# An SSM and feed-forward mix on one core: x's transposes in queues of their own, and a planner with measured durations

## The chip, the cores and the metric

The kernel runs on one core of one Trainium2 chip. Times are device microseconds of one execution; the time of a kernel is the median of its runs. Engines are named as in the profile: PE is TensorE, DVE VectorE, ACT ScalarE, POOL GpSimd, SP SyncE, which here issues the transfers.

## The reference

```python
def _A_ref(u, log_A_real, A_imag, C_real, C_imag, log_dt, D_skip):
    dt = jnp.exp(log_dt)
    A = -jnp.exp(log_A_real) + 1j * A_imag
    C = (C_real + 1j * C_imag) * dt[:, None]
    P = jnp.exp((A * dt[:, None])[:, :, None] * pos[None, None, :])
    K = 2.0 * jnp.einsum("dn,dnl->dl", C, P).real      # taps of a long filter
    ...                                                # y = u convolved with K along L, per channel
    return y + u * D_skip[None, None, :]

def _B_ref(x, w1, w2):
    return jnp.einsum("bsf,fd->bsd", jnp.maximum(jnp.einsum("bsd,df->bsf", x, w1), 0), w2)

x = A_u                                                # 1 x 2048 x 640, float32
g = _sigmoid((x * gate_w).sum(-1, keepdims=True))
return g * _A_ref(x, ...) + (1 - g) * _B_ref(x, w1, w2)   # w1 640 x 1728, w2 1728 x 640; N = 128
```

The convolution over 2048 positions is done with transforms of length 2048 in two factors, as products with tables.

## The kernel before

**Two halves of work, woven together.** The feed-forward half runs in three passes over the hidden columns (5, 5 and 4 blocks of 128, one of them 64 wide), and in each over eight groups of 256 rows of x. Products are made in float32 accuracy from a rounded high part and a low remainder of each operand: three products for one. In the first pass a group's x is loaded (`xu`), transposed on PE in three blocks of 2, 2 and 1 column tiles (`trans`, into the PSUM tile `pk`, of which there is one; for group 0 also `px`, `pg`), cast by ACT to the high part and subtracted by DVE to the low part (`xx`, two sets by turns), and stored to DRAM (`xt`) for the later passes. Then come the hidden products (`hidden` in the first pass, `wide` in the others: `pf<-xx,w1`), relu by ACT (`hh`) and its remainder by DVE (`hl`), and four runs of output products (`sums`: `pf<-w2,hh`, 320 wide), each evicted to `q`. Between passes q goes through DRAM (`part`): it is stored at a group's end and loaded again (`load_q`) in the next pass; there are two q buffers. In the last pass ACT first scales the loaded q by 1 - g (`q<-q,omg`), and what is finished goes to the output.

**The other half** makes the taps and convolves. 40 chunks of channels give phases and exponents on PE (`pg`, `px`, `pe`), then cosines, sines, exponentials and products on ACT and DVE (`cs`, `sn`, `mg`, `me`, `G`); two chunks together make taps on PE (`taps`, into `pk`), turned by DVE (`kt`), and stored (`kd`). The convolution then goes over five slices of 128 channels, in stages on PE, all into the PSUM tiles `pc`, of which there are three: `tf` (first factor of the transform, of the taps `ck`/`cl` and of the input `xu`), `tm`, pointwise products on ACT, DVE and POOL, `tn`, a turn on DVE (`relay`), and `tw`: eight products in four pairs for a slice (`inv1`). A pair is multiplied by the gate on ACT into one of five `yo` buffers, and either stored to DRAM (`y`), to be added to q later, or joined by POOL with what pass three has left in `part` (loaded as `yj`), and stored to the output.

**The planner.** No order is written out. Every step is a `Task` with an engine, a queue, a duration that the author estimates (`dur`), what it depends on, and tokens of the buffers that it takes. `Plan.run` simulates the engines with these durations and emits the program in the simulated order: tasks of one queue stay in the order in which they were added, and between the heads of an engine's queues the one with the lowest `rank` goes first among those that are ready. Transfers have one line of time, `dma`, that each moves on by its `kb` over a rate. A change of kind on PE (`mode`: 'f' for full products, 'c' for convolution, 't' for taps) costs `CHANGE`. On the chip the engines run by themselves: each takes its instructions strictly in the emitted order and waits at the one that isn't ready. All instructions are recorded by one helper, so all rows of the profile have its line, L314; the tile names tell what they are.

Of the kernel before, what the change touches and what calls it, by code (L numbers as in the profile page):

```python
# [51 lines left out]
GPR = 1  # L52
GTR = 3
# [88 lines left out]
class Plan:  # L142
# [5 lines left out]
    FETCH = 2.4  # L148
    BUSY = 2.6
    SLACK = .8  # L150
    BURST, GATHER, PATIENCE = ('c', 'c1'), 2, 3

    def __init__(self):
# [68 lines left out]
    def run(self):  # L222
        self.free = {e: 0.0 for e in self.LAG}
        mode, dma, log, done, block, since = {}, 0.0, [], 50.0, 0.0, 0.0
        heads = {k: 0 for k in self.queues}
        while True:
            best = None
            for e in self.LAG:
                c, soon = [], []
                for (eng, q), n in heads.items():  # L230
                    if eng == e and n < len(self.queues[eng, q]):
                        t = self.queues[eng, q][n]
                        r, known = self.ready(t)
                        for g in t.glue:
                            r2, k2 = self.ready(g)
                            r, known = max(r, r2), known and k2
                            for b in t.take:
                                k = sum(x.ring is b.ring for x in (*t.take, *g.take))
                                r = max(r, sorted(b.ring.slots)[k - 1] if len(b.ring.slots) >= k else 1e9)
                        (c if known else soon).append((r, t))  # L240
                if not c:
                    continue
                at = max(self.free[e], min(r for r, _ in c))
                key = lambda t: t.prio + (0.5 if t.mode is not None and mode.get(e) not in (None, t.mode) else 0)
                r, t = min((x for x in c if x[0] <= at), key=lambda x: key(x[1]))
                start = max(at, r)
                if e == 'PE' and mode.get(e) == 'f':


                    if t.mode in self.BURST and at - since < self.PATIENCE and self.burst(c, heads, at) < self.GATHER:  # L250
                        other = [x for x in c if x[1].mode == 'f' and x[0] <= at + .05]
                        if other:
                            r, t = min(other, key=lambda x: key(x[1]))
                            start = max(at, r)
                if e == 'PE' and (t.mode != 'f' or mode.get(e) != 'f'):

                    for r2, t2 in c:
                        if key(t2) < key(t) and r2 <= at + self.HOLD:
                            t, start = t2, max(at, r2)
                    hold = [r2 for r2, t2 in soon if t2.prio < t.prio and r2 <= at + self.HOLD]  # L260
                    if hold:
                        at = max(hold)
                if best is None or at < best[0]:
                    best = at, e, t, start
            if best is None:
                break
            _, e, t, start = best
            change = self.CHANGE.get(e, 0) if t.mode is not None and mode.get(e) not in (None, t.mode) else 0
            if e == 'PE' and t.mode != 'f':
                since = start + t.dur  # L270
            if t.mode is not None:
                mode[e] = t.mode
            for b in t.take:
                b.ring.slots.remove(min(b.ring.slots))
            t.fn()
            self.free[e] = start + change + t.dur
            if e == 'PE':

                done += t.n
                while done >= 128:  # L280
                    done -= 128
                    at = self.free[e] - t.dur * done / t.n
                    fetch = self.FETCH + (self.BUSY if dma > at + 2 else 0)
                    self.free[e] += max(0, block + fetch - at)
                    block = max(at, block + fetch)
            if t.port:

                self.free[e] += 0.25 * min(max(self.free['POOL'] - start, 0), t.dur)
            t.end = self.free[e] + t.lag
            if t.kb:  # L290
                dma = max(dma, start + min(t.dur, 0.62) + 0.5) + t.kb / (230 if start < 12 else 270)
                t.end = max(dma, start + t.dur) + 1.1
            for b in (*t.take, *t.use):
                b.left -= 1
                b.free = max(b.free, t.end)
                if b.left == 0:
                    b.ring.slots.append(b.free)
            heads[e, t.q] += 1
            log.append((start, t))
        stuck = [(k, self.queues[k][n]) for k, n in heads.items() if n < len(self.queues[k])]  # L300
        assert not stuck, [(k, len(self.queues[k]) - heads[k]) for k, _ in stuck]
        self.log = log
# [42 lines left out]
class Kernel:  # L345
# [30 lines left out]
    def feed_forward(self):  # L376
        A, nc, V, S, P, D_ = self.plan.add, self.nc, self.V, self.S, self.P, self.D
# [11 lines left out]
        parts, k = [], 0  # L389
# [5 lines left out]
        st = {}  # L395
# [90 lines left out]
        def trans(g, third, src):  # L486
            s_, ld = src
            bank = ('pk', 'px', 'pg')[0 if g else third]
            b_ = tok(bank)
# [18 lines left out]
            def low():  # L508
                V.tensor_sub(st['x', g][1][:, k0:k0 + kn], st.pop(('xb', g, third))[:, :kn],
                             st['x', g][0][:, k0:k0 + kn].bitcast(F32))  # L510
            a = A('PE', 'ff', 0.22 * kn, pe, [ld], take=[b_], use=[s_], mode='f')
            b = A('ACT', 'ff', 0.12 + 0.2 * kn, high, [a], take=[x_] if third == 0 else (),
                  use=[b_] if third == 0 else [b_, x_], rank=0)
            c = A('DVE', 'ff', 0.08 + 0.27 * kn, low, [b], use=[b_, x_], rank=0)
            X.setdefault((0, g), []).extend((b, c))
            self.x_read.append(a)

# [93 lines left out]
        def wide(p, P, f):  # L611
# [30 lines left out]
            def low():  # L642
                V.scalar_tensor_tensor(st['hw', f][1], st.pop(('hb', p, P, f)), 0.0, st['hw', f][0].bitcast(F32), op0=ALU.max,
                                       op1=ALU.subtract)
            wt, w_ = W[p, f, 0]
            ts = [A('PE', 'ff', 0.69, pe(k), [*wt, *xd_], take=() if k else [b_], use=[w_, *xs_] + ([b_] if k else []),
                    mode='f', n=3) for k in range(NT)]
            a = A('ACT', 'ff', 0.52, high, [*ts, *(self.zs if p == 1 and f > 1 else ())], take=[h_], use=[b_], rank=0)
            b = A('DVE', 'ff', 0.62, low, [a], use=[b_, h_], rank=0)
# [141 lines left out]
        for p, n in enumerate(PARTS):  # L791
# [3 lines left out]
            for k, g in enumerate(order):  # L795
# [28 lines left out]
                if not last:  # L824
                    es = [sums(p, g, j, q_, qld) for j in range(4)]

                    def store(p=p, g=g):
                        D_.dma_start(sc['part'][p % 2][g], st['q', g])
                    done[p, g] = A('SP', 'st', 0.62, store, es, use=[q_], kb=640, rank=6, late=True)
                    continue  # L830
                if k % 2 == 0 and k < 6:
                    paced = [x for i in order[k + 2:k + 4] for x in X[p, i]]
# [179 lines left out]
    def ssm(self, C=16):  # L1012
# [26 lines left out]
        st = {}  # L1039
# [25 lines left out]
        def phases(c):  # L1065
            p_, s_ = tok('pg'), tok('sc')
            rd, r_ = rows[c]

            def pe():
                p = self.psg.tile([128, 4, 256], F32, name="pg")  # L1070
                pf = p.rearrange("p d j -> p (d j)")
                st['pg'] = pf.rearrange("p (d j) -> p d j", j=64)
                for h in range(2):
                    x = slice(h * 512, h * 512 + 512)
                    self.E.matmul(pf[:, x], R[c], self.tg[:, x], start=True, stop=True)

            def whole():
                st['sc', c] = [st['gp'].tile([128, C, 64], F32, name=k, bufs=5) for k in ("sn", "cs")]
                S.copy(I(st['sc', c][1]), st['pg'])
            a = visit[c, 1] = A('PE', None, 0.5, pe, [rd, opened, *self.tg_done], take=[p_], use=[r_], rank=GPR, mode='f')  # L1080
            b = acts[c, 0] = A('ACT', None, 0.97, whole, [a], take=[s_], use=[p_], rank=2)
            d = A('DVE', 'g1', 1.14, lambda: V.tensor_sub(st['sc', c][0], st['pg'], I(st['sc', c][1])), [b],
                  use=[p_, s_], rank=G1R)
            e = A('DVE', 'g1', 0.62, lambda: V.tensor_scalar(I(st['sc', c][1]), I(st['sc', c][0]), 0x7fffffff, None,
                                                             op0=ALU.bitwise_and), [d], use=[s_], rank=G1R, port=True)
            tasks[c] = dict(s=s_, abs=e)

        def exponents(c):
# [13 lines left out]
            def exps(k):  # L1102
# [5 lines left out]
                        st['me', c] = st['gp'].tile([128, C, 32], F32, name="me", bufs=4)  # L1108
                        S.activation(st['me', c], st.pop(('pe', c)), AF.Exp)
                return go  # L1110
            a = visit[c, 2] = A('PE', None, 0.7, pe, [rd, opened, *self.tg_done], take=[p_], use=[r_], rank=GPR, mode='f')
            b = acts[c, 1] = A('ACT', None, 0.52, exps(0), [a], take=[m_], use=[p_], rank=2, mode='exp')
            d = acts[c, 2] = A('ACT', None, 0.96, exps(1), [b], use=[p_, m_], rank=2, mode='exp')
            s_ = tasks[c]['s']
# [39 lines left out]
        def taps(p):  # L1154
# [17 lines left out]
            def out():  # L1172
                kt = st.pop(('kt', p))
                for j in range(4):
                    d0 = 2 * (p * C + j * Q)
                    D_.dma_start(self.sc['kd'][:, d0:d0 + 2 * Q, :].rearrange("(h a) d b -> a h (d b)", h=2),
                                 kt[32 * j:32 * j + 32].rearrange("p h q b -> p h (q b)"))
            a = visit[p, 0] = A('PE', None, 2.0, pe, [*w[0]['f'], *w[1]['f']], take=[b_], use=us, rank=GTR, mode='t', n=128)
            b = A('DVE', 'g5', 0.65, turn, [a], take=[k_], use=[b_], rank=G5R)
            d = A('POOL', 'g5', 0.6, lambda: P.tensor_add(st['kt', p][:, 1, :, 0], st['kt', p][:, 1, :, 0], dsk[:, p]),  # L1180
                  [b, sk], use=[k_])
# [359 lines left out]
```

## Time and profile before

| | |
|---|---|
| median of 3 runs | 644.29 us (642.56 to 644.78) |
| profiled execution | 642.35 us, its span 640.6 us |
| PE, DVE, ACT, POOL busy | 617.3, 508.5, 402.1, 93.9 us |
| moved by DMA | 107.78 MB |

Of the span, roughly the first 95 us are pass one of the feed-forward half with the parameters of the taps on DVE; to some 405 us the taps are made beside passes one and two; from then on the convolution runs beside passes two and three. In a row of the timeline the time in brackets is how long the engine had been idle, and who ended that. PE's products overlap, so their own durations add up to more than the time they take; runs of them are read from the chain.

### The profile page before, as it was taken

The page shows a single profiled execution, that of the slowest core. Times are in us where ns is not written, and L with a number is a line of the kernel's source. Part 1 is how long each engine was busy: PE and PEld are TensorE (multiplying, and loading weights), DVE is VectorE, ACT ScalarE, POOL GpSimd, SP SyncE. Part 2 cuts the span into 40 slices and gives each one's busy share as a digit, 9 for nine tenths or more (in the row PEclk, how much of TensorE's full clock was granted, in tenths as well). Part 3 has the DMA queues.
Part 4 walks back from the last instruction along what each step waited for, and adds up shares of the span by engine and source line. Part 5 has one row for each costly group of instructions (what it writes and reads, how often), then busy time and mean ns, then how long its engine had stood idle before and what let it go on. Part 6 is the DMA issues. An engine that isn't in the chain of part 4 may idle for free.

```text
span 640.6 us, 19212 instructions
## 1 busy us (share of the span) xinstructions
PE 617.3 (96%) x8236; PEld 503.0 (79%) x8236; DVE 508.5 (79%) x818; ACT 402.1 (63%) x603; POOL 93.9 (15%) x134
## 2 busy tenths in 40 slices
PE   7989999899999899999999999999999999999897
PEld 6989998798898798898898898665565556756577
DVE  4889936989999999998999999768579753966542
ACT  5557439999999988988978985113443424432550
POOL 0000000000000000000000000024151531713633
PEclk9999999999999999999999999999999999999999
DMA  9974774333456734373454225794406558156355
GB/s 256 326 236 147 221 229 165 105 125 112 136 167 210 255 122 144 122 242 117 129 198 154 79 80 176 258 315 132 144 3 215 185 164 263 53 158 188 102 166 133
DMA packets 76176, 107.78 MB, mean 168 GB/s; under 512 B 7610, under 2 KB 58682, under 8 KB 75195
## 3 DMA queue, kind: packets, MB, share of 16 engines
q1 hardware_dynamic: 75930, 106.14, 53.2%
q8 instruction: 65, 1.06, 0.7%
q10 hardware_dynamic: 160, 0.41, 0.3%
q14 instruction: 21, 0.16, 0.1%
HBM read 67.47 MB, written 44.30 MB: 174 GB/s over the span
## 4 chain that ended last, share of the span: by engine, by line
PE 56%; DVE 5%; DMA 2%; ACT 2%; issue 1%; SPq 1%; DVEq 0%; ACTq 0%
PE pf L314 35%; PE pc L314 13%; PE pk L314 4%; DVE ku L314 3%; PE pg L314 2%; PE px L314 2%; DMA part<-q 1%; ACT ku L314 1%; PE pe L314 1%; DMA out_dram<-yo 1%; SPq L314 1%; DVE sn L314 1%; ACT cs L314 0%; DVE q L314 0%; ACT q L314 0%
## 5 line engine op out<-in xcount | busy, mean ns | idle before, releaser
L314 PE MATMUL pf<-xx,w1h 128*128 128x256 f32 (+1 forms) x760 | 184.2, 339 | 0.4 <-DVE xx L314 0.3
L314 PEld LDWEIGHTS pf<-xx,w1h 128*128 128x128 f32 x760 | 125.2, 189 | 22.8 <-issue 7.3
L314 PE MATMUL pf<-xx,w1l 128*128 128x512 f32 (+1 forms) x340 | 115.7, 340 | 0.0
L314 PE MATMUL pf<-w2h,hh 128*128 128x320 f32 x288 | 89.7, 315 | 2.4 <-DVE hl L314 1.5
L314 PE MATMUL pf<-w2l,hh 128*128 128x320 f32 x288 | 87.8, 309 | 0.0
L314 ACT COPY ku<-pc 128x512 f32<-128x512 f32 (+1 forms) x60 | 43.8, 761 | 68.2 <-PE pc L314 56.7
L314 PE MATMUL pf<-w2h,hl 128*128 128x320 f32 x256 | 73.3, 312 | 0.0
L314 PEld LDWEIGHTS pf<-xx,w1l 128*128 128x128 f32 x340 | 64.3, 189 | 7.6 <-DVE w1l L314 0.2
L314 POOL TENSOR_TENSOR kt<-kt,dsk 128x8 f32<-128x8 f32 x20 | 10.3, 515 | 392.7 <-DVE kt L314 377.8
L314 POOL TENSOR_TENSOR ku<-ku 128x256 f32<-128x256 f32 x80 | 56.2, 737 | 55.3 <-DVE ku L314 49.1
L314 DVE TENSOR_TENSOR ku<-pc,ku 128x512 f32<-128x512 f32 x80 | 52.6, 684 | 12.5 <-ACT ku L314 11.3
L314 DVE STREAM_TRANSPOSE ku<-pc 128x512 f32<-128x512 f32 x80 | 50.2, 683 | 13.7 <-PE pc L314 13.7
L314 PEld LDWEIGHTS pf<-w2h,hh 128*128 128x128 f32 x288 | 54.1, 188 | 7.7 <-issue 3.7
L314 DVE TENSOR_TENSOR sn<-pg,cs 128x1024 f32<-128x1024 f32 x40 | 48.7, 1217 | 7.5 <-ACT cs L314 7.5
L314 PEld LDWEIGHTS pf<-w2l,hh 128*128 128x128 f32 x288 | 54.1, 188 | 0.6
L314 ACT ACT_TABLE_LOAD x42 | 53.9, 1283 | 0.7
L314 ACT CAST cs<-pg 128x1024 int32<-128x1024 f32 x40 | 40.3, 1008 | 21.2 <-PE pg L314 21.0
L314 DVE TENSOR_TENSOR mg<-mg,cs 128x1024 f32<-128x1024 f32 x40 | 48.9, 1222 | 1.3
L314 PEld LDWEIGHTS pf<-w2h,hl 128*128 128x128 f32 x256 | 46.4, 188 | 3.5 <-issue 2.9
L314 PE MATMUL pc<-ku,tm 64*32 64x256 f32 x1280 | 42.2, 392 | 3.6 <-DVE ku L314 2.4
L314 ACT ACTIVATE cs<-cs,half_pi 128x1024 f32<-128x1024 f32 x40 | 45.6, 1140 | 0.0
L314 ACT ACTIVATE hh<-pf 128x512 fp32r<-128x512 f32 (+1 forms) x40 | 20.5, 513 | 39.4 <-PE pf L314 39.4
(170 smaller groups left out, 1232.5 us busy)
## 6 DMA issues: line engine op xcount, KB each, us to landing
xx<-xt SPq DMA_DIRECT2D x24, 640.0 KB, 6.8
xt<-xx SPq DMA_DIRECT2D x16, 640.0 KB, 3.9
part<-q SPq DMA_DIRECT2D x16, 640.0 KB, 3.4
q<-part SPq DMA_DIRECT2D x16, 640.0 KB, 5.3
ws<-in_B_w_dram SPq DMA_DIRECT2D x20, 320.0 KB, 5.5
kd<-kt SPq DMA_DIRECT2D x80, 64.0 KB, 1.8
ub<-in_A_u_dram SPq DMA_DIRECT2D x10, 512.0 KB, 4.7
xu<-ub SPq DMA_DIRECT2D x5, 1024.0 KB, 6.2
```

Source lines behind the costliest of these rows:

```text
L314: self._last = self._tc.keep_in_program_order(f(*a, **k))
```

## The change

The three steps of `trans` move from the queue `ff`, in which they stood in one order with all products, casts and remainders of the feed-forward half, to a queue `xp` on each of PE, ACT and DVE; on PE with rank 4.5, while the products have 5. So a block of transposes is placed as soon as the simulation has its inputs and the buffer `pk` ready, wherever the products are. The other edits change numbers of the simulation: durations on PE of a wide product (0.69 to 0.681), of phases (0.5 to 0.46), exponents (0.7 to 0.69) and taps (2.0 to 1.83), half the cost of a change of kind that involves taps, and the transfers: a task of several transfers is now simulated as so many, each 0.62 us after the other, with rates by queue instead of 270 (230 in the first 12 us), and 1.27 us to land instead of 1.1.

```diff
+    RATE = dict(x=330, q=287, st=320, yq=200, y4=260, mx=297, cu=215, kd=231, ub=401, xt=485, rows=697, prm=215, tab=340, tab0=171)
...
+            if e == 'PE' and 't' in (t.mode, mode.get(e)):
+                change /= 2
...
             if t.kb:
-                dma = max(dma, start + min(t.dur, 0.62) + 0.5) + t.kb / (230 if start < 12 else 270)
-                t.end = max(dma, start + t.dur) + 1.1
+                m = max(1, round(t.dur / 0.625))
+                for j in range(m):
+                    dma = max(dma, start + 0.62 * j + 1.15) + t.kb / m / self.RATE.get(t.q, 250)
+                t.end = max(dma, start + t.dur) + 1.27
...
-            a = A('PE', 'ff', 0.22 * kn, pe, [ld], take=[b_], use=[s_], mode='f')
-            b = A('ACT', 'ff', 0.12 + 0.2 * kn, high, [a], take=[x_] if third == 0 else (),
+            a = A('PE', 'xp', 0.22 * kn, pe, [ld], take=[b_], use=[s_], rank=4.5, mode='f')
+            b = A('ACT', 'xp', 0.12 + 0.2 * kn, high, [a], take=[x_] if third == 0 else (),
                   use=[b_] if third == 0 else [b_, x_], rank=0)
-            c = A('DVE', 'ff', 0.08 + 0.27 * kn, low, [b], use=[b_, x_], rank=0)
+            c = A('DVE', 'xp', 0.08 + 0.27 * kn, low, [b], use=[b_, x_], rank=0)
...
-            ts = [A('PE', 'ff', 0.69, pe(k), [*wt, *xd_], take=() if k else [b_], use=[w_, *xs_] + ([b_] if k else []),
+            ts = [A('PE', 'ff', 0.681, pe(k), [*wt, *xd_], take=() if k else [b_], use=[w_, *xs_] + ([b_] if k else []),
...
-                    done[p, g] = A('SP', 'st', 0.62, store, es, use=[q_], kb=640, rank=6, late=True)
+                    done[p, g] = A('SP', 'st', 0.62, store, es, use=[q_], kb=310, rank=6, late=True)
...
-            a = visit[c, 1] = A('PE', None, 0.5, pe, ...
+            a = visit[c, 1] = A('PE', None, 0.46, pe, ...
...
-            a = visit[p, 0] = A('PE', None, 2.0, pe, ...
+            a = visit[p, 0] = A('PE', None, 1.83, pe, ...
```

Since the simulation sets the whole order, nearly every row of every engine moves a little. Three places follow.

**DVE in the first pass, at the subtractions for group 2 before and group 3 now** (`xx` is a subtraction of x's remainder, `hl` one of the hidden layer, `ra` and `sa` steps of the parameters' exponential, `logit` the gate's sum). Before:

```order
L314 SCALAR_TENSOR_TENSOR sa<-sa,ra 128x640 x2
L314 SCALAR_TENSOR_TENSOR hl_560<-pf,hh_559 128x512
L314 TENSOR_TENSOR xx<-pk,xx 128x512
L314 SCALAR_TENSOR_TENSOR sa<-sa,ra 128x640
L314 SCALAR_TENSOR_TENSOR hl_587<-pf,hh_586 128x256
L314 TENSOR_TENSOR xx<-pk,xx 128x256
```

Now:

```order
L319 SCALAR_TENSOR_TENSOR hl_597<-pf,hh_596 128x256
L319 SCALAR_TENSOR_TENSOR ra<-ni,ra 128x640
L319 TENSOR_SCALAR sa<-ra 128x640
L319 TENSOR_TENSOR xx<-pk,xx 128x512
L319 SCALAR_TENSOR_TENSOR sa<-sa,ra 128x640 x4
L319 TENSOR_TENSOR xx<-pk,xx 128x512
L319 SCALAR_TENSOR_TENSOR sa<-sa,ra 128x640 x2
L319 SCALAR_TENSOR_TENSOR xu,logit<-xu,gw 128x640
L319 TENSOR_TENSOR xx<-pk,xx 128x256
```

Before, each subtraction of x came behind the remainder of the hidden block that was made beside it; now group 3's three stand among the parameter steps, while PE makes the output products of group 1. On PE the blocks of transposes stand accordingly: before between hidden products, 30 and 15 of them apart, now between output products. This is the first block of group 3 now (`w2h,hl` and the like are output products):

```order
L319 MATMUL pf<-w2h_276,hl_512 128x320
L319 MATMUL pf<-w2h_299,hl_564 128x320
L319 MATMUL pk<-ident,xu 128x128 x4
L319 MATMUL pf<-w2h_314,hl_564 128x320
L319 MATMUL pf<-w2h_351,hl_597 128x320
```

Before, the last block of a group stood behind its last hidden products and ahead of the first output products.

**SP in the last pass, at the end of group 4** (`part_4<-q` is its second store, `q<-part_6` the load of group 6 into the same buffer, `yj` loads for the joins). Before:

```order
L314 DMA out_dram<-q 64x256 x2
L314 DMA part_4_72<-q 128x384
L314 DMA yj<-part_4_72 128x2x128
L314 DMA yj<-part_0_68 128x2x128
L314 DMA yj<-part_1_69 128x2x128
L314 DMA yj<-part_2_70 128x2x128
L314 DMA yj<-part_3_71 128x2x128
L314 DMA q<-part_6_82 128x1280
```

Now:

```order
L319 DMA part_4_72<-q 128x384
L319 DMA yj<-part_4_72 128x2x128
L319 DMA q<-part_6_82 128x1280
L319 DMA yj<-part_0_68 128x2x128
L319 DMA yj<-part_1_69 128x2x128
L319 DMA out_dram<-yo 64x4x128 x2
L319 DMA yj<-part_2_70 128x2x128
```

The load of q has moved ahead of four loads of yj.

**ACT at the multiplications of the `tw` products of slices 2 and 3** (`yo<-pc,gate`, four rows to a pair; `ku<-pc` are casts of other convolution stages). Before:

```order
L314 COPY ku<-pc 128x4x128x2 x4
L314 ACTIVATE yo<-pc,gate 128x128 x24
L314 COPY ku<-pc 128x512 x3
L314 ACTIVATE q<-q,omg 128x640
L314 COPY ku<-pc 128x512
L314 ACTIVATE q<-q,omg 128x640
L314 COPY ku<-pc 128x512 x4
L314 ACTIVATE yo<-pc,gate 128x128 x8
```

Now:

```order
L319 COPY ku<-pc 128x4x128x2 x4
L319 ACTIVATE yo<-pc,gate 128x128 x12
L319 ACTIVATE q<-q,omg 128x640
L319 ACTIVATE yo<-pc,gate 128x128 x12
L319 ACTIVATE q<-q,omg 128x640
L319 ACTIVATE yo<-pc,gate 128x128 x8
L319 COPY ku<-pc 128x512 x6
```

The two scalings of group 6's q stood between casts of the `tm` stage; now they stand inside the multiplications. On PE the `tw` products, before 6, 2, 4 and 4 rows for these two slices with other work between, are now 6 and 10, with 20 output products between:

```order
L319 MATMUL pf<-w2h_5350,w2l_7315 128x320
L319 MATMUL pc<-ku,tw 64x512 x10
L319 MATMUL pc<-ck,tf 64x512 x4
L319 MATMUL pc<-xu,tf 64x512 x16
L319 MATMUL pc<-cl,tf 64x512 x4
```

For slices 0 and 1 it is the same (before 6, 2, 4 and 4, now 6 and 10).

More of the change, by code (lines that the diff above doesn't have):

```diff
@@ L1079, in whole @@
                 S.copy(I(st['sc', c][1]), st['pg'])
-            a = visit[c, 1] = A('PE', None, 0.5, pe, [rd, opened, *self.tg_done], take=[p_], use=[r_], rank=GPR, mode='f')
+            a = visit[c, 1] = A('PE', None, 0.46, pe, [rd, opened, *self.tg_done], take=[p_], use=[r_], rank=GPR, mode='f')
             b = acts[c, 0] = A('ACT', None, 0.97, whole, [a], take=[s_], use=[p_], rank=2)
@@ L1110, in exps @@
                 return go
-            a = visit[c, 2] = A('PE', None, 0.7, pe, [rd, opened, *self.tg_done], take=[p_], use=[r_], rank=GPR, mode='f')
+            a = visit[c, 2] = A('PE', None, 0.69, pe, [rd, opened, *self.tg_done], take=[p_], use=[r_], rank=GPR, mode='f')
             b = acts[c, 1] = A('ACT', None, 0.52, exps(0), [a], take=[m_], use=[p_], rank=2, mode='exp')
@@ L1177, in out @@
                                  kt[32 * j:32 * j + 32].rearrange("p h q b -> p h (q b)"))
-            a = visit[p, 0] = A('PE', None, 2.0, pe, [*w[0]['f'], *w[1]['f']], take=[b_], use=us, rank=GTR, mode='t', n=128)
+            a = visit[p, 0] = A('PE', None, 1.83, pe, [*w[0]['f'], *w[1]['f']], take=[b_], use=us, rank=GTR, mode='t', n=128)
             b = A('DVE', 'g5', 0.65, turn, [a], take=[k_], use=[b_], rank=G5R)
```

## The prediction

> **What bounds the kernel now.** I read the page first: its span, its busy row and its clock row.
>
> ```profile
> span 640.6 us, 19212 instructions
> PE 617.3 (96%) x8236; PEld 503.0 (79%) x8236; DVE 508.5 (79%) x818; ACT 402.1 (63%) x603; POOL 93.9 (15%) x134
> PEclk9999999999999999999999999999999999999999
> ```
>
> TensorE (PE) is busy for 617.3 of 640.6 us at the full granted clock, and the change neither adds nor removes a product. So the time is PE's work plus what PE waits. The table of busy time by stage says who could make it wait (columns: window, PE, PEld, DVE, ACT, POOL busy with counts, clock, DMA share, GB/s):
>
> ```profile
> 0.00:40.00 40.00, 35.10 (x248) 32.95 (x248) 28.00 (x65) 20.06 (x38) 0.87 (x7) 1.00 0.95 281
> 160.00:200.00 40.00, 38.47 (x462) 34.57 (x460) 39.22 (x61) 37.44 (x50) 1.14 (x2) 1.00 0.56 174
> 560.00:600.00 40.00, 37.25 (x555) 20.98 (x553) 28.31 (x48) 15.45 (x40) 16.56 (x20) 1.00 0.54 157
> ```
>
> The first stage has slack on VectorE (DVE) and ScalarE (ACT), the tap stage has next to none (39.22 of 40 on DVE), the convolution has slack again but waits on chains through DMA. The view of waits, cut to PE, is the whole budget:
>
> ```profile
> PE pk L314 <- DVE xx L314: 5.6, 5, 1.7
> PE pc L314 <- DVE ku L314: 3.1, 6, 1.7
> PE pk L314 <- DMA xu<-in_A_u_dram: 2.3, 2, 1.1
> PE pg L314 <- DVE sn L314: 2.1, 1, 2.1
> PE pf L314 <- DVE hl L314: 1.5, 1, 1.5
> PE pe L314 <- POOL ident masks.py:199: 1.5, 1, 1.5
> PE pc L314 <- ACT ku L314: 1.0, 1, 1.0
> PE pf L314 <- ACT hh L314: 0.9, 1, 0.9
> ```
>
> These eight add up to 18.0 us. The 1.5 at the start and one of the two 1.1 on the first load stay in any order, so a reordering can win at most about 15 us; what it can lose has no such ceiling. Before and after, PE's order leaves its matrix products 37 times for convolution pieces and 20 times for taps, so switching costs the same.
>
> **Part 1: x's transposes in queues of their own.** The largest row above, 5.6 us in 5 waits, is one pattern. The timeline around the longest:
>
> ```profile
> 36.82 0.66 PE L314 MATMUL pk<-ident,xu 128*128 128x128 f32 x4
> 37.51 0.59 ACT L314 CAST xx<-pk 128x512 fp32r<-128x512 f32 x1
> 37.53 0.49 DVE L314 TENSOR_SCALAR sa<-ra 128x640 f32<-128x640 f32 x1
> 38.05 1.68 DVE L314 SCALAR_TENSOR_TENSOR sa<-sa,ra 128x640 f32<-128x640 f32 x2
> 39.66 0.68 DVE L314 SCALAR_TENSOR_TENSOR hl<-pf,hh 128x512 fp32r<-128x512 f32 x1
> 40.26 0.68 DVE L314 TENSOR_TENSOR xx<-pk,xx 128x512 fp32r<-128x512 f32 x1
> 40.99 0.44 PE L314 MATMUL pk<-ident,xu 128*128 128x128 f32 x2 [1.74 <-DVE xx L314]
> ```
>
> The buffer pk is single. The second block of transposes is cast by ACT at 37.51, but DVE subtracts only at 40.26, behind parameter steps (sa) and the hidden layer's hl. The third block stands 15 products further on PE: 40.99 - 1.74 - 36.82 = 2.43 us for four transposes and 15 products, so some 2.0 us of cover against a round trip of 40.94 - 37.2 = 3.7 us.
>
> In the new order the blocks of groups 3 to 7 stand among the output products of a group, 12, 16 and 19 of them apart. A run of such products gives the price:
>
> ```profile
> 623.67 13.12 PE pf L314 x88
> 620.01 3.65 PE pc L314 x16
> 603.34 2.02 PE pc L314 x124
> ```
>
> 13.12 / 88 = 0.149 us each, so the cover becomes 1.8, 2.4 and 2.8 us, where cast and subtraction alone are 0.59 + 0.68 and some 0.3 of hand-over, 1.6 us. For group 3, DVE now has the first xx, four sa steps (4 x 0.84 = 3.4, half of the 1.68 row each), then the second xx: ready about 5.9 us after the first block starts, with the third block due at 0.4 + 2.4 + 0.4 + 2.8 = 6.0 (0.4 for four transposes, 2.43 less 2.0 above). That just fits. I leave 0.8 of the 5.6 in place: -4.8 us. Bounds: 0 (the waits come back behind other DVE steps) to -5.6.
>
> Further waits of that stage:
>
> ```profile
> 13.47 0.63 PE L314 MATMUL pk<-ident,xu 128*128 128x128 f32 x4 [1.15 <-DMA xu<-in_A_u_dram]
> 99.31 0.41 PE L314 MATMUL pf<-w2h,hh 128*128 128x320 f32 x1 [0.89 <-ACT hh L314]
> 175.45 0.41 PE L314 MATMUL pf<-w2h,hh 128*128 128x320 f32 x1 [1.53 <-DVE hl L314]
> ```
>
> The first waits for group 1's load. Twelve more hidden products now stand ahead of it, 12 x 2.0 / 15 = 1.6 us, more than the wait: -1.1 (bounds 0, -1.15). The loads in SyncE's queue stand in the same order up to there. The other two are the step from a group's hidden products to its output products. At the later one a tap (2 us) now stands between most of the hidden products and the outputs, at the earlier one a phase product and a tap follow the first four. But at groups 2 and 3 the two transposes that stood in this step are gone and x's cast is ahead of the last hidden cast on ACT, which can cost some 0.5 each. Of 2.4 I take -1.0 (bounds +1, -2.4).
>
> **Part 2: the new costs in the tap stage.** Shorter phases, taps and products let the planner put more PE work ahead of each DVE step. Counted in PE's own work, the first convolution product comes about 6 us later than before; the last group's x blocks stand some 17 us earlier, out of the busiest stretch. DVE is at 39.22 of 40, so a late DVE step can hit PE anywhere; before, this happened once, at pg (2.1). I take -1.0 (bounds +3, -2.1).
>
> **Part 3: the convolution and its transfers.** The worst place of before:
>
> ```profile
> 583.35 3.49 SPq L314 DMA_DIRECT2D yj<-part  x5
> 586.94 0.54 SPq L314 DMA_DIRECT2D q<-part  x1
> 591.83 0.83 ACT L314 ACTIVATE q<-q,omg 128x640 f32<-128x640 f32 x1 [4.96 <-DMA out_dram<-yo]
> 592.56 0.56 ACT L314 COPY ku<-pc 128x512 f32<-128x512 f32 x1
> 594.72 1.15 PE L314 MATMUL pc<-ku,tm 64*32 64x256 f32 x32 [1.70 <-DVE ku L314]
> ```
>
> SyncE issues five yj loads before group 6's q load; ACT's in-order queue stands 4.96 us at the scaling of q (the view names another transfer, the q load is what it reads); the casts behind it come late, and PE waits 1.70, then 0.50, 0.17 and 0.24 at the next steps. In the new order that q load stands behind one yj load instead of five, 4 x 0.7 = 2.8 us sooner, and no cast of that stage stands behind it: -2.6, and with the similar 1.0 at 457 us -3.6 (bounds 0, -4.4).
>
> What comes instead: the last convolution products (tw, four pairs for each of five slices) of slices 0 and 1, and of 2 and 3, now stand in one burst each, six and ten products with 20 output products between, and the scaling of q for groups 4 and 6 stands inside the burst in ACT's queue. Prices:
>
> ```profile
> 574.45 0.53 DVE q L314
> 576.53 6.80 DMA part<-q
> 621.19 3.21 ACT L314 ACTIVATE yo<-pc,gate 128x128 f32<-128x128 f32 x12 [1.83 <-PE pc L314]
> part<-q SPq DMA_DIRECT2D x16, 640.0 KB, 3.4
> q<-part SPq DMA_DIRECT2D x16, 640.0 KB, 5.3
> ```
>
> Group 6's q load needs the buffer of group 4, so it waits until group 4's last store has landed. From group 4's last product to that store's issue are 576.53 - 574.45 = 2.1 us and 0.1 before it, landing takes 3.4 (median) to 6.8 (here), two issues 1.2, the load 5.3: data at 12.0 to 15.4 us. PE gets there sooner: four products 0.6, the tn products 2.0, three pairs 3 x 0.91 (3.65 / 4) = 2.7, 20 products 3.0, buffer waits and switches about 0.9, then three more pairs into the three PSUM buffers: 12.0. The next pair needs a buffer that ACT empties only after scaling q (0.83) and four multiplications (3.21 / 3 = 1.07): at 13.9 to 17.3 instead of 12.0. So 1.9 to 5.3 us, in each of the two bursts. In slice 0's burst the scaling stands one pair later, but three yj loads stand ahead of its q load. I take 2.5 each, near the median landing, because fewer other transfers stand ahead of the store than at 576: +5.0. Bounds: 0 (the data is there) to +16, where the five yo buffers, freed only by stores behind these loads in SyncE's queue, add a few us to each.
>
> **Sum.** -4.8 - 1.1 - 1.0 - 1.0 - 3.6 + 5.0 = -6.5 us. Against the profiled execution's 642.35 us that is 635.9; that execution lies 1.9 us below the median of the three runs, 644.29, so I forecast **637.8** as median. The tail is as before: after the last tw products PE has 62 products (9.2 us) instead of 88, and ACT's 16 multiplications behind them take 4.4.
>
> **Rivals.** *A, slower: the bursts of tw products.* The same mechanism at its upper price, 8 us a burst instead of 2.5: group 4's store lands after 6.8 us as it did at 576, and the yo stores queue behind the yj loads on SyncE. -6.5 + 11 = +4.5, so 648.8. It decides from a landing of some 6 us on. For it: ACT did stand 4.96 us at just this scaling. Against: another such store, issued at 504.08, let its reader start at 508.90, as the transfers were fewer.
>
> ```profile
> 504.08 0.33 SPq L314 DMA_DIRECT2D part<-q  x1
> 508.90 1.88 SPq L314 DMA_DIRECT2D yj<-part  x3
> ```
>
> A wait of PE in one piece of over 3.4 us would, by the Trainium skill, "TensorE: Matmul & The Clock Gate", section "HAM oscillation", drop the clock to half for a window of 3.4 us, worth about 1.7 us more in each burst by an estimate from that page: 652 instead of 649. No wait of this trace is that long and its clock row never drops, so no run here shows it so far; I give it 3 of A's 20 in 100.
>
> *B, same: DVE takes it back.* The tap stage runs at DVE's pace, so PE time won before 160 us is waited away between 160 and 400 at pg, pk and pf: the gains of part 1 (6.9) vanish, the rest nets to +0.4, so 644.7. For: 39.22 of 40. Against: PE waited only 2.1 us in 200 us of that stage, as other products fill in, and the new order has those too.
>
> *C, better: the q data is in time and all waits of part 1 go.* -6.5 - 5.0 - 0.8 - 1.4 = -13.7, so 630.6. For: transfers are now costed nearer to what the page shows. Against: ACT is the slower one inside a burst anyway.
>
> That the change doesn't do what it says is excluded by the order: the transposes do stand elsewhere.
>
> **Numbers.** Forecast 0.50 (634 to 642), A 0.20, B 0.16, C 0.14. The range 630 to 647 takes in B and the upper half of C, and leaves out two thirds of A and C's lower half, 0.2 in all. About 0.3% (1.9 us) is what a measurement of this kernel can tell: faster is the forecast and C, 0.64; same is B, 0.16; slower is A, 0.20.
>
> **What would show it.** In the waits view "PE pk <- DVE xx" falls from 5.6 to under 1.5, and "DMA xu" to one wait of 1.1. The row at 594.72 has no successor: tm products run without a wait over 0.5. In the two bursts ACT stands before a scaling of q for 1 to 3 us and PE waits 2 to 4 us nearby. The step from hidden to output products costs 1 to 2 us in all. I am wrong if the first 160 us still hold 6 us of PE waits, if the bursts show none or over 5 us each, or if PE's waits between 160 and 400 us exceed 4 us.

## The result, and the profile after

The changed kernel takes 641.23 us (median of 22 runs) against 643.40 us for the kernel before (22 runs): a ratio of 0.997, 95% interval 0.9957 to 0.9983. That is 1.9 us less (1.1 to 2.8 by the interval) where I had forecast 6.5. The time itself lies inside the forecast's 634 to 642, but that is luck, as the band is wide: the change is about a third of what was forecast. The profiled execution took 640.79 us with a span of 639.0.

The first page of the changed kernel, span and busy row:

```profile
span 639.0 us, 19204 instructions
PE 619.6 (97%) x8236; PEld 504.4 (79%) x8236; DVE 508.8 (80%) x818; ACT 402.4 (63%) x603; POOL 93.2 (15%) x134
```

Its table of busy time by stage, the three stretches that were shown of before (columns: window, PE, PEld, DVE, ACT, POOL busy with counts, clock, DMA share, GB/s):

```profile
0.00:40.00 40.00, 37.68 (x267) 35.74 (x267) 28.29 (x69) 22.81 (x51) 0.87 (x7) 1.00 0.97 293
160.00:200.00 40.00, 39.06 (x566) 34.27 (x566) 38.98 (x55) 37.36 (x48) 1.84 (x3) 1.00 0.54 165
560.00:600.00 40.00, 36.83 (x494) 19.78 (x500) 24.15 (x41) 17.16 (x44) 12.43 (x14) 1.00 0.52 146
```

The first stage has gained (37.68 us busy instead of 35.10), the last has not. And PE is busy for 619.6 us instead of 617.3 with the same 8236 products, which the prediction had no term for. The view of waits, cut to PE (total us, times, longest), without the wait for ident that is unchanged; "issue" is a stop for which the profile names no releaser:

```profile
PE pc L319 <- ACT yo L319: 4.2, 3, 2.4
PE px L319 <- ACT mg L319: 2.3, 3, 1.2
PE pf L319 <- issue: 1.9, 1, 1.9
PE pf L319 <- DVE hl L319: 1.3, 3, 0.9
PE pf L319 <- DVE q L319: 1.1, 1, 1.1
PE pc L319 <- issue: 0.5, 1, 0.5
PE pk L319 <- DVE cs L319: 0.4, 1, 0.4
PE pc L319 <- DVE ku L319: 0.3, 2, 0.2
PE pf L319 <- DVE xx L319: 0.3, 1, 0.3
PE pk L319 <- DMA xu<-in_A_u_dram: 0.3, 1, 0.3
PE pk L319 <- DVE xx L319: 0.2, 1, 0.2
PE pk L319 <- DVE sn L319: 0.2, 1, 0.2
PE pc L319 <- ACT ku L319: 0.2, 1, 0.2
```

Of the rows that led before, xx, xu and ku are all but gone. The first row is the price of the bursts. Two things are new: a stop of 1.9 us with no releaser but "issue", and px waiting for ACT.

The first burst in the timeline, SyncE's queue, then ACT, then PE (columns: start, duration, engine; in brackets the idle time before and its releaser):

```profile
484.60 1.87 SPq L319 DMA_DIRECT2D yj<-part  x3
486.51 0.60 SPq L319 DMA_DIRECT2D q<-part  x1
492.89 0.83 ACT L319 ACTIVATE q<-q,omg 128x640 f32<-128x640 f32 x1 [1.86 <-DMA q<-part]
494.80 1.08 PE L319 MATMUL pc<-ku,tw 128*64 128x512 f32 x4 [2.38 <-ACT yo L319]
```

Three yj loads are issued ahead of the q load; ACT stands 1.86 us at the scaling of q, and PE 2.38 us behind ACT, inside the burst. The other burst, at 574 to 578 us, costs 1.17 and 0.66.

The stop without a releaser, in PE's timeline:

```profile
476.50 0.31 PE L319 MATMUL pf<-w2l,w1h 128*128 128x320 f32 x1
478.71 0.31 PE L319 MATMUL pf<-w2h,w1l 128*128 128x320 f32 x1 [1.90 <-issue]
```

And the extra busy time. The timeline of PE shows three waits close together:

```profile
205.73 0.72 PE L319 MATMUL px<-tg,PS 128*128 128x512 f32 x2 [1.17 <-ACT mg L319]
207.36 0.32 PE L319 MATMUL pk<-mg,cs 128*32 128x64 f32 x2 [0.44 <-DVE cs L319]
207.96 0.32 PE L319 MATMUL pk<-G,sn 128*32 128x64 f32 x2 [0.16 <-DVE sn L319]
```

The table of busy time by single microseconds behind them (the clock stands third from the end of a row):

```profile
207.00:208.00 1.00, 0.48 (x12) 0.24 (x14) 1.00 (x3) 1.00 (x2) 0.00 (x0) 0.70 1.05 420
208.00:209.00 1.00, 1.00 (x40) 1.00 (x44) 1.00 (x1) 0.98 (x2) 0.00 (x0) 0.50 0.99 389
209.00:210.00 1.00, 1.00 (x50) 1.00 (x45) 0.97 (x3) 0.99 (x2) 0.00 (x0) 0.50 1.00 415
210.00:211.00 1.00, 1.00 (x49) 1.00 (x40) 1.00 (x2) 1.00 (x2) 0.00 (x0) 0.60 1.05 435
```

Soon after these waits the granted clock is 0.50 for 3.4 us (from 207.39 us): 0.30 + 0.50 + 0.50 + 0.40 = 1.7 us lost, in a group of 128 taps that took 2 us before.

### The profile page after: what moved, and what is told of

The parts are those of the page before. It is cut to its first block, busy times and chain, and to the rows that moved or that the text cites. A ratio compares the mean times of both kernels' runs of the same rounds, so it can differ in the third digit from the quotient of the medians.

```text
span 639.0 us, 19204 instructions
## 1 busy us (share of the span) xinstructions
PE 619.6 (97%) x8236; PEld 504.4 (79%) x8236; DVE 508.8 (80%) x818; ACT 402.4 (63%) x603; POOL 93.2 (15%) x134
## 4 chain that ended last, share of the span: by engine, by line
PE 74%; DVE 12%; DMA 5%; ACT 4%; issue 3%; SPq 1%; POOL 0%; ACTq 0%; DVEq 0%
PE pf L319 48%; PE pc L319 13%; PE pk L319 7%; PE px L319 2%; PE pg L319 2%; DVE sn L319 2%; DVE G L319 1%; DMA part<-q 1%; DVE ku L319 1%; DVE hl L319 1%; DVE mg L319 1%; PE pe L319 1%; SPq L319 1%; DVE cs L319 1%; DMA out_dram<-yo 1%
## 5 line engine op out<-in xcount | busy, mean ns | idle before, releaser
L319 PE MATMUL pf<-w2h,hl 128*128 128x320 f32 x256 | 75.1, 315 | 1.1 <-DVE hl L319 1.1
L319 ACT ACTIVATE sn<-sn 128x1024 f32<-128x1024 f32 x40 | 42.2, 1055 | 0.2
```

The source lines that it names most:

```text
L319: self._last = self._tc.keep_in_program_order(f(*a, **k))
```

## Experiments

All kernels were timed beside the kernel before on the same chip; the ratios are to it. "Order frozen" means that the list of the planner's tasks is written out and only the named tasks are moved, so that nothing else shifts. My theory was that the terms of the sum stand and that what it missed sits in few places: the stop, the bursts, the half clock.

### The changed kernel again (order frozen)

```diff
+ORDER = [...]          # the task numbers in the order that the planner chose
+for k in ORDER: tasks[k].fn()
```

> The changed kernel once more, its planner's order written out as a list of task numbers (same instructions in the same order on each engine). Theory 1 (each loss sits in the order): PE's stop of 1.9 us at 476 us with no releaser named, the half clock at 207 to 210 us (1.7 us lost) and the two waits at the tw bursts (2.4 and 1.2 us) stand in the new trace at the same places; time 641.2. Rival (chance of one execution): the stop and the half clock are elsewhere or gone, the waits at the bursts stay, and such an execution takes 637 to 638.

642.63 us, 0.9987 (0.9962 to 1.0012): the gain is so small that this set alone can't tell it from none. In the timeline of PE the stop stands at the same product:

```profile
480.35 0.30 PE L362 MATMUL pf<-w2h,w1l 128*128 128x320 f32 x1 [1.69 <-issue]
```

In the view of waits the bursts are there again:

```profile
PE pc L362 <- ACT yo L362: 4.4, 2, 2.2
```

The half clock is elsewhere, in the table by single microseconds:

```profile
494.00:495.00 1.00, 0.00 (x0) 0.00 (x0) 0.00 (x0) 0.92 (x2) 0.00 (x0) 1.00 1.05 308
496.00:497.00 1.00, 1.00 (x4) 0.29 (x4) 0.00 (x0) 1.00 (x5) 0.98 (x1) 0.50 0.51 141
```

So the stop and the waits belong to the order. The half clock differs between executions of one order: here the wait of 1.2 at px passed without it, and the two bursts were followed by it (from 496 and from 578 us).

### One part at a time

Queues alone:

```diff
-a = A('PE', 'ff', 0.22 * kn, pe, [ld], take=[b_], use=[s_], mode='f')
+a = A('PE', 'xp', 0.22 * kn, pe, [ld], take=[b_], use=[s_], rank=4.5, mode='f')
... (cast and subtraction likewise; no cost changed)
```

> The kernel before with x's transposes, casts and subtractions in queues of their own, and all planner costs as before. Theory 1 (the early stage's gain is kept to the end): PE's waits for xx and for xu's load fall from 7.9 to under 1 us as in the changed kernel, and the time falls by 5 to 8 us, to 635 to 638, less what a shifted convolution adds. Rival 2 (the tap stage runs at DVE's pace and takes it back): the same waits go from the first 160 us, but PE waits as much more between 160 and 400, and the time stays at 642 to 644.

642.46 us, 0.9977 (0.9957 to 0.9997). The time is the rival's, the mechanism isn't: PE's idle time between 160 and 400 us did not grow (240 less 237.06 = 2.9 us, before 3.9). xx fell from 5.6 to 0.5, but other steps came late in their place, PE stopped for 2.0 us without a releaser (at 540 us), and the profiled execution had the half clock after 160 and for 7 us from 211; the mean granted clock of the 12 runs was 0.9937, the kernel before's 0.9977. Its view of waits:

```profile
PE pg L314 <- DVE sn L314: 3.5, 2, 2.1
PE pc L314 <- issue: 2.4, 2, 2.0
PE px L314 <- ACT mg L314: 1.7, 3, 0.8
PE pc L314 <- ACT ku L314: 1.5, 2, 1.3
PE pk L314 <- DVE xx L314: 0.5, 1, 0.5
```

Costs alone:

```diff
-a = A('PE', 'xp', 0.22 * kn, pe, [ld], take=[b_], use=[s_], rank=4.5, mode='f')
+a = A('PE', 'ff', 0.22 * kn, pe, [ld], take=[b_], use=[s_], mode='f')
... (cast and subtraction likewise; all new costs kept)
```

> The changed kernel with x's transposes, casts and subtractions back in the common queue, all new costs kept. Its tw products stand in the same five groups of rows as before (6 and 2, 4, 4 for a pair of slices), not in bursts of ten. Theory 1: the 5.6 us of waits for xx and about 2 us for xu stay, the waits of 4.1 us for ku may go: 639 to 643. Rival 2 (the gain of the change is the convolution's, not x's): 640 to 641, no slower than the changed kernel.

656.03 us, 1.0198 (1.0163 to 1.0232): both expectations were wrong. The waits for xx grew to 6.2 with one of 2.6, and PE's busy time to 625.3 us, with the half clock at 43 to 46 and 224 to 231 us. From its view of waits:

```profile
PE pk L319 <- DVE xx L319: 6.2, 5, 2.6
PE px L319 <- ACT mg L319: 3.3, 3, 1.8
PE pc L319 <- DVE ku L319: 2.6, 8, 0.8
```

The parts don't add: -0.2%, +2.0%, and -0.3% together. Costs and queues together give another order than either alone, so neither run prices its half of the change.

### The convolution's order against the early order

The order of the changed kernel up to the planner's 394 us, then that of the kernel before; and the reverse.

```diff
+ORDER = after[:1655] + [k for k in before if k not in after[:1655]]    # and the reverse: before[:1660] + rest of after
```

> The order of the changed kernel up to the planner's 394 us (the first 1655 of its tasks, everything before the convolution), then the order of the kernel before for all that is left; only five tasks lie differently at the seam. Theory 1 (the early gain lasts, the new convolution costs 3 to 4 us): 636 to 638, with the first 400 us as in the changed kernel and the waits for ku of some 4 us back after it. Rival 2 (the tap stage takes the early gain back): 641 or more, and PE's gaps up to 400 us as many as before.

643.37 us, 1.0015 (0.9998 to 1.0031). At first sight rival 2. The timeline of PE shows a fault of the experiment: at the seam one group of taps stood too early.

```profile
399.99 0.32 PE L362 MATMUL pk<-mg,cs 128*32 128x64 f32 x2 [3.16 <-DVE cs L362]
```

This wait, the half clock from 399.8 to 403.2 behind it and the one from 208 are all in that execution.

> The reverse: the order of the kernel before up to the seam, then that of the changed kernel. Theory 1: the early waits stay, the bursts of tw products and the stop near 476 us come in: before plus 3 to 4 us, 646 to 647. Rival 2 (the convolution's new order is what brings the gain): at or below 642.

647.19 us, 1.0061 (1.0040 to 1.0082), as theory 1 expected: on the old beginning the new convolution costs 0.6%, 3.9 us. Its view of waits has the old ones of the beginning beside the new ones of the end:

```profile
PE pk L362 <- DVE xx L362: 5.6, 5, 1.7
PE pc L362 <- ACT yo L362: 4.2, 3, 1.9
PE pf L362 <- issue: 1.5, 1, 1.5
```

The seam mended: the group of taps (task 769) five groups of products later.

```diff
-769, 2217, 770, 2220, 771, 2221, 772, 2222, 2223
+2217, 2220, 2221, 2222, 2223, 769, 770, 771, 772
```

> The first part of the changed kernel's order and the convolution of the kernel before, as in the first such run, but with the one group of taps at the seam, which stood 3.2 us at a sum on DVE there, put five groups of products later on PE. Theory 1 (the early gain of some 7 us in PE's gaps lasts, and the seam hid it): 637 to 639.5. Rival 2 (the tap stage and the clock take it back): 641 or more again.

639.13 us, 0.9925 (0.9898 to 0.9952): theory 1. The new order up to 394 us is worth 0.75%, some 4.8 us (interval 3.1 to 6.6), and rival B of the prediction (the tap stage takes it back) falls: PE's idle time between 160 and 400 us is 3.6 us, before 3.9. Part of the 4.2 us between this run and the one with the faulty seam is the clock: its mean over the runs is 0.9988 here and 0.9949 there, by an estimate 2.5 of 640 us. In the profile of this run, which has no half clock at all, PE's idle time is 637.2 - 619.5 = 17.7 us (before 23.3), but PE is busy for 619.5 us instead of 617.3. What these 2.2 us are stays open.

### The bursts

```diff
-ts.append([A('ACT', 'mx', 0.76, lambda t=t, b=b: S.mul(st['q', g][:, t], ..., self.omg[:, b:b + 1]), ...)])
+ts.append([A('POOL', 'mx', 0.76, lambda t=t, b=b: P.tensor_scalar_mul(st['q', g][:, t], ..., self.omg[:, b:b + 1]), ...)])
-YO = 5
+YO = 8
```

> The changed kernel in its own order, written out, with q's scaling by omg moved from ACT to POOL (same place in the list) and eight yo buffers instead of five. Theory 1 (ACT stands at the scaling of q in the middle of a burst of tw products, and PE waits for the PSUM buffers behind it): PE's waits for yo of 4.2 us fall under 1 us, and the time falls by 3 to 5 us from the changed kernel's, to 636 to 638. Rival 3 (the burst is limited by ACT's multiplications or the waits move to POOL and DVE's q): within 1.5 us of the changed kernel.

643.53 us, 0.9984 (0.9965 to 1.0004). The waits for yo are gone from the list. Two things were changed at once, so this run doesn't tell whether the scaling on ACT or the number of yo buffers made them; the next one does. The time is rival 3's: scaling takes 1.96 us on POOL (0.83 on ACT), and PE waits for DVE's additions to q, which wait for POOL's (and these for the load of y). The scaling's row in the groups of instructions (count, busy us, mean ns, idle before):

```profile
L362 POOL TENSOR_SCALAR q<-q,omg 128x640 f32<-128x640 f32 x16 | 31.2, 1955 | 10.0 <-DMA out_dram<-yo 6.1 <-DMA q<-part 3.9
```

And its view of waits:

```profile
PE pf L362 <- DVE q L362: 2.5, 2, 2.3
PE pc L362 <- DMA ck<-kd: 1.3, 1, 1.3
```

The cheaper cure is SyncE's order (frozen order, two loads moved):

```diff
+DMA q<-part
 DMA yj<-part x3
-DMA q<-part
```

> The changed kernel in its own order, with the two loads of q that ACT's scaling inside the bursts waits for put ahead of the yj loads in SyncE's queue (three yj loads at the first burst, one at the second). Theory 1 (those loads are late by SyncE's order): q lands about 1.9 and 0.7 us sooner, PE's waits for yo fall from 4.3 to about 2 us, and the time falls by 2 to 2.5 us. Rival 3 (q's buffer, freed by the landing of the store, sets it, or the yj loads then hold up the yo buffers): under 1 us.

639.84 us, 0.9945 (0.9924 to 0.9965), 1.4 to 2.8 us below the changed kernel's two medians, about what theory 1 had, though the intervals of the ratios overlap. With five yo buffers and the scaling on ACT as before, the waits for yo fell, so the late q loads made most of them. The view of waits (4.2 before the move):

```profile
PE pc L362 <- ACT yo L362: 1.7, 3, 1.0
```

### The stop without a releaser

The trace holds 65 transfers of 16 KB on queue 8, marked as instructions, for PE's 8236 products: one for 127. In the changed kernel one of them starts at 476.44, 231 products after the one before it, and PE goes on 2.3 us after its start. From 472.6 to that moment the DMA engines move a reload of x and a store of q.

> The changed kernel in its own order, with two reloads of x (640 KB each, issued at 471.7 and 479.5 us, first read at 509) moved in SyncE's queue behind the loads for the first burst, to about 494 us. Theory 4 (PE's stop of 1.9 us near 477 us is its own instruction load, the 16 KB on queue 8 that comes at 476.4 instead of about 472 because the data of this reload is ahead of it on the DMA engines): that load comes at 472 to 474, the stop falls under 0.7 us, and the time falls by 1 to 2 us. Rival 5 (the stop comes from the 128 short products before it, whatever the DMA engines do): the stop stays at 1.7 to 1.9 us at the same product.

What ran is not quite that: in the list the two reloads came to stand far ahead, and were issued at 270 us. So some of the later products work on another group's x; the time is that of a convolution without these two transfers at 472 to 485. 638.61 us, 0.9933 (0.9910 to 0.9956). The instruction load came 140 products after the last one, and in the timeline of PE the stop has shrunk:

```profile
479.32 0.31 PE L362 MATMUL pf<-w2h,w1l 128*128 128x320 f32 x1 [0.27 <-issue]
```

The reloads at their intended kind of place:

```diff
-DMA xx<-xt
 DMA part<-q
-DMA xx<-xt
 ...
 DMA ck<-kd, cl<-kd            # at 497 to 500 us
+DMA xx<-xt x2
```

> The changed kernel in its own order, with the two reloads of x that are issued at 471.7 and 479.5 us moved in SyncE's queue behind the four loads of kernel pieces at 497 to 500 us (x is first read at 509). Theory 4 (PE's own instruction load is held up by this data): the stop of 1.7 to 1.9 us near 477 falls under 0.7, and the time is 1 to 2 us below the changed kernel's, 639 to 640.5. Rival 5 (the density of short products alone): the stop stays.

The stop is gone altogether (the instruction load now comes 99 products after the last, at product 5803 instead of 5935), so theory 4 holds for this place. But the time is 641.97 us, 0.9972 (0.9946 to 0.9998): the two reloads, 1.3 MB, now delay the load of u behind them in the same queue, PE waits there, and the half clock followed it from 512 us. In the timeline of PE:

```profile
512.19 1.45 PE L362 MATMUL pc<-xu,tf 64*64 64x512 f32 x8 [2.31 <-DMA xu<-ub]
```

> The changed kernel with both moves in SyncE's queue: the two q loads ahead of the yj loads, and the two reloads of x behind the loads at 500 us. If the two losses are separate, their gains add: 637 to 638.5. If the loads of q and the reloads only trade places on the DMA engines, it stays at 639.5 to 640.

640.78 us, 0.9957 (0.9936 to 0.9979): neither forecast. Both cures work at their place, no stop and 2.0 us for yo, and the wait for u has grown to 3.2. In the view of waits:

```profile
PE pc L362 <- DMA xu<-ub: 3.2, 1, 3.2
PE pc L362 <- ACT yo L362: 2.0, 4, 0.7
```

### The best of both

The mended kernel with four q loads put ahead of the yj loads next to them:

```diff
 ORDER = head_mended, with
-yj ..., q
+q, yj ...                     # four times in the last pass
```

> The mended kernel of both orders, with the four q loads of the convolution's last pass put ahead of the yj loads next to them in SyncE's queue. Theory 1: the casts behind the scaling of q on ACT come in time, PE's waits for ku of some 3.7 us fall to about 1, and the time is 2 to 3 us below that of the mended kernel. Rival 3 (the landing of the store sets it): under 1 us.

637.20 us, 0.9894 (0.9866 to 0.9923), the fastest kernel of this study, 1.9 us below the mended one by its median, though the two intervals overlap and the two profiled executions have the same span (637.3 and 637.2); so this last gain is not shown. The waits for ku were 1.8 behind ACT and 1.7 behind DVE in the mended kernel; the first, at 456 us, is down to 0.3, and a new one of 1.1 stands at 616. Its view of waits:

```profile
PE px L362 <- ACT mg L362: 2.6, 4, 1.2
PE pc L362 <- DVE ku L362: 1.9, 4, 1.1
```

## Why the prediction was wrong

*The priced terms.* Each can be read off the two views of waits, forecast first. Waits for xx: -4.8, measured 0.2 - 5.6 = -5.4. First load of x: -1.1, measured 0.3 - 2.3 = -2.0 (in the repeated run -1.0). Hidden to output products: -1.0, measured 1.3 - 2.4 = -1.1. Tap stage: -1.0, measured +0.8: pg's 2.1 is gone, but px waits 2.3 and the taps 0.6, so this sign was wrong. Casts of ku: -3.6, measured 0.5 - 4.1 = -3.6. Bursts: +5.0, measured 4.2 for yo, +4.2, at the low end of the 1.9 to 5.3 a burst that had been worked out (here 2.4 and 1.8). The 1.1 for q stands at 584 us, behind the second burst, where DVE waits for POOL's addition and that for the load of y; with it +5.3. Together -6.0 where I had -6.5. None of the signs that I had named for being wrong came either (PE's idle time is 4.1 us in the first 160 us and 2.9 between 160 and 400): they all watch waits that were in the list.

*The step that failed* is the first: "the time is PE's work plus what PE waits", with the work as a constant and eight named waits as "the whole budget". Two costs had next to no row in the trace of before, and got neither a term nor a rival. One is the stop: "issue" rose from 0.3 to 2.4, +2.1 us, within one product of the same place in the five profiles with this convolution and its x reloads in place. The other is PE's own busy time, +2.3, of which 1.7 are the half clock at 207 to 211; the other 0.6 have no cause shown, and busy times of 619.5 us in the mended kernel and 620.8 in the fastest one, both without any half clock, say that more than the clock can lengthen it. -6.0 + 2.1 + 2.3 = -1.6, and the two profiled executions differ by 640.79 - 642.35 = -1.56. The first cost could have been asked for: the planner of both kernels has a term that reads like it (`FETCH` and `BUSY` in the kernel: after every 128 products PE is held until 2.4 us after the block before, 5.0 when the simulated transfers are over 2 us behind), and the change alters the simulated transfers that this goes by.

*The clock.* I used the rule of the Trainium skill, "TensorE: Matmul & The Clock Gate", section "HAM oscillation", that gaps of PE over 3.4 us drop the clock, and so spoke of it in rival A alone. The price that I estimated with that figure, 1.7 us for one drop, is what the rows above show. The threshold does not hold here: the drops of these profiles followed single waits of 1.2 to 3.2 us, none of 3.4. The Trainium skill says on the same page, section "What's actually happening", that activity is watched in a free-running window. The traces agree: in each of the 14 all changes of the granted clock lie a whole number of stretches of 3.413 us apart, counted from its first rise (at 4.3 to 7.6 us, other in each execution). What goes with a drop is how much of such a stretch PE stands in all. Up to PE's last product, PE stood idle for over 60% of the time in nine stretches, and the full clock fell behind each; for 45 to 52% in eighteen, and it fell behind eight; for less in all the others, and it fell behind none of those. What decides between 45 and 52% stays open. The wait of 1.17 us at px shows it in one order. In five of the ten profiles that have this beginning it lies in one stretch with the waits behind it, 1.55 to 1.68 us in all, and a drop follows. In the other five the stretches end so that none holds more than 1.36 us, and none follows. The table by such stretches, for the changed kernel (a drop at its end) and for the mended one (none at either end):

```profile
203.98:207.39 3.41, 1.80 (x14) 0.80 (x13) 3.41 (x6) 3.27 (x6) 0.00 (x0) 1.00 0.80 273
203.04:206.45 3.41, 2.24 (x12) 1.64 (x11) 3.38 (x5) 3.40 (x6) 0.00 (x0) 1.00 0.44 153
206.45:209.87 3.42, 2.76 (x131) 2.08 (x129) 3.39 (x5) 3.25 (x5) 0.00 (x0) 1.00 1.01 406
```

So where the stretches lie in an execution is chance, and the cost shows in means: the mean granted clock was 0.9977, 0.9977 and 0.9975 in the kernel before's three sets of runs here, 0.9965 and 0.9955 in the changed kernel's two. On 640 us that is 1.5 us against 2.2 to 2.9, about 1 us of the gain. This is read from what goes with what; no run took the clock alone away.

*The rivals.* A was wrong in its size: its 8 us a burst is not the 5.3 at which its own working ends, and no burst cost 5 us. B is refuted by the mended kernel. C's condition, the q data in time, could be had by moving the q loads, not by the planner's costs.

*The convolution's sign* was right (+1.4 in the sum, measured -3.6 + 5.3 = +1.7, and with the stop +3.8; the reverse kernel cost 3.9). So of a gain of 4 to 5 us at the beginning more than half was given back at the end, where the largest losses, the waits for yo and the stop, go with the order of transfers in SyncE's one queue.

## What to carry to other kernels

A change to a planner's costs is a new program. Price the new waits stage by stage, and where the stages can be cut apart, keep the better order of each: here the new beginning with the old convolution gained 0.75%, where the change as a whole gained 0.3%. Ask of every product-dense stretch whether the engine's own instruction loads come in time next to large transfers, and add up the matrix engine's waits that lie close together: here 1.6 us of them within 3.4 us could cost 1.7 us more by the clock. Where one in-order queue issues a load that an engine is about to stand at, put it ahead of those that nobody waits for yet, and look which load then comes late.

## What was unexpected of the hardware

PE's instructions come as 16 KB transfers, 65 for 8236 products, and the page of the profile counts them on the same 16 DMA engines as the data. With 960 KB of reload and store in the way one came some 130 products later than without (product 5935 against 5803), and PE stopped for 1.5 to 1.95 us. Two other kernels fit. With the new costs alone PE stopped for 1.66 us at 444 us, when the DMA engines were quiet, but a load had come only at 438.75, 240 products after its predecessor, behind two reloads and a store, and the next at 442.86. With the queues alone it stopped for 1.98 us at 540, 2.5 us after the start of a load that came 177 products after its predecessor.

The granted clock fell to 0.50 for 3.4 us, twice for 6.8, in 11 of 14 profiles. In these traces it goes with the sum of PE's waits in a stretch of 3.4 us whose phase is set anew in each execution, and not with the length of one wait: the kernel before had waits of up to 2.1 us in its profile, at most 51% of a stretch, and no drop.
